# Strassen downs: where the weight sums, the g sums, two state sections and the last recombination stand in a one-core kernel

## The chip, the cores and the metric

The kernel runs on one core of a Trainium2 chip. A core has five engines that each run their own program in order: TensorE (PE, matmuls, with its weight loads shown apart as PEld), VectorE (DVE), ScalarE (ACT), GpSimd (POOL) and SyncE (SP), which here issues all loads, transposes and stores as DMAs. Engines wait for one another by semaphores only. SBUF is the on-chip memory that all engines read, PSUM the small accumulator memory of eight banks (128 x 512 float32 each) that PE writes.

The metric is the device time of one execution in microseconds (us), the median over the runs of a kernel. Profiled executions carry a span, from the first to the last recorded instruction or transfer, and all times "at 91.77" are measured from the span's start.

## The reference

Linear attention with decay over 4 batches, 8 heads, 768 positions and 64 dimensions, in blocks of 64, and then a feed-forward layer over the 3072 tokens:

```
for b in range(nb):                                   # per head, blocks of 64
    intra = ((qb @ kb.T) * Dmask) @ vb                # Dmask: lam**(i-j) below the diagonal
    inter = (qb * lam_pow) @ kv_state
    out[block b] = intra + inter
    kv_state = lam_block * kv_state + (kb * rev_pow).T @ vb
x = out as 3072 x 512
h = x @ w_in                                          # 512 x 2048
g = h * (1 / (1 + exp(-h)))                           # SiLU
return g @ w_out                                      # 2048 x 512
```

Inputs and output are float32.

## The kernel before

The tokens are cut into 24 chunks of 128 (two blocks of 64 for all eight heads; the chunks of one batch follow each other, six to a batch) and into 12 groups of 256 tokens, so group g holds chunks 2g and 2g+1. All matmul operands are cast to bf16. The order of all instructions is written by hand: the program order of the code is the order in which each engine runs its own part.

**Attention.** Chunks 0 to 3 run in an opening written out as a table of words; the later ones run in `section()` (L438 to L574). For a chunk, POOL multiplies q and k by their decays (`qb`, L364, `kb`, L365; together a "prep"), SP issues DMA transposes of them into `qt` (L390) and `kn` (L391), and PE makes scores `sp`, states `kv_ps` and outputs `op`, all in 64 x 64 matmuls recorded on L540. DVE masks the scores (`ss`, L560) and adds the states up (`total`, L570 and L572); the running state is cast to bf16 (`kvs`, by `move`: ACT L178, POOL L180 or DVE L182). Values are cast by `vcast` (`vb`, ACT). The output of a chunk is cast into `xt`. For two chunks the transposes are made on PE instead (`pe_tk`, matmuls L413, copied to `kn` by DVE). `first_state()` (L579 to L589) prepares the state for the first chunk after the opening on DVE.

**Feed-forward, up.** For each group, `ups(g, i)` for i from 0 to 7 runs eight matmuls of 128 x 256 (L604) into a PSUM bank, which gives two slices of 128 of the 2048 hidden columns for the 256 tokens of the group, and ACT applies SiLU (L609, 0.60 us each) into a tile `g`.

**Feed-forward, down.** Groups 0 and 1 use plain products (`down0`, `ffn2`, matmuls L643). Groups 2 to 11 use Strassen's scheme on halves of the tokens and of the hidden and output columns: seven products of eight matmuls each (128 x 256, L711) in place of eight. This needs sums of w_out (`weight_sum`, L669 to L677: five sums, each in two halves of 128 x 1024, on DVE, L674) and sums of g (`g_sums`, L680 to L700, after each unit, on DVE): `gd` (L693) for products 6 and 7, `gc` (L689) for product 1, `gb` (L691) for products 5 and 2. For i below 4 only `gd` is made; for i from 4 to 7 `gc`, `gb` and `gd`.

`seven(g)` (L713 to L767) runs the products in the order 3, 4, 1, 6, 5, 2, 7. Two PSUM banks hold them, `o[0]` and `o[1]`, in halves of 256 columns. After product 4, ACT copies the first half of `o[0]` to `m` (msum, L733) and DVE adds the second (L734); after 6, DVE adds product 1 (L737); products 5 and 2 are then accumulated on top of 3 and 4 in `o[0]`, so product 5 waits until msum is read out. After 2, ACT copies `o[0]` (L740) and DVE subtracts it from `m` for two quarters of the output (L741); after 7, DVE adds `o[1]` (L753). For the last group, product 7 has a tile of its own, `o_tail` (L750); four stores, one for each quarter, are issued by SP in `put` (L726).

**The order around it.** The loop over g from 2 to 10 (L907 to L939) runs eight units of `ups` and then the seven products; before the product at place 2 the loop issues preps, transposes and loads for chunks ahead, and for groups 2 and 3 a section with the scores and states of chunks 2g+2 and 2g+3; before the one at place 5 a section with the outputs of chunks 2g+2 and 2g+3 and (from group 3 on) the scores and states of the next two. Group 11 comes last with nothing behind it. Ahead of the loop, w_out arrives in six loads of 512 KB in the order 0 to 5 (two of its eight pairs of slices come later); each is cast by `cast_w` (L856 to L857, on DVE). Then come loads and preps of chunks 4 to 7, `first_state()` and the first half of the five weight sums (L865 to L866); their other half stands at L896 to L897.

`gpool` (26 buffers) holds all g tiles and g sums, each of 512 bf16 values per partition.

Of the kernel before, what the change touches and what calls it, by code (L numbers as in the profile page):

```python
# [7 lines left out]
F32 = mybir.dt.float32  # L8
# [28 lines left out]
def kernel(  # L37
# [29 lines left out]
    gpool = ctx.enter_context(tc.tile_pool(name="gpool", bufs=26))  # L67
# [370 lines left out]
    def section(outs=(), scores=(), states=(), e="AA", tags=(("att", 3),) * 2, spare=None, cast="D"):  # L438
# [126 lines left out]
        for c, h in states:  # L565
            b = c // NB
            kvs = nat.tile([128, NP, D], BF16, name="kvs", tag="kvs", bufs=8)
            old, total[b] = total.get(b), nat.tile([128, NP, D], F32, name="total", tag="total", bufs=4)
            if old is None:
                nc.vector.tensor_copy(total[b], place(c, h))  # L570
            else:
                nc.vector.tensor_tensor(total[b], old, place(c, h), op=AL.add)  # L572
            move(cast, kvs, total[b])
            kvh[(c, 1) if h == 0 else (c + 1, 0)] = kvs  # L574
# [31 lines left out]

    def ffn1_close(g, i):
        gg = gpool.tile([128, 2, 256], BF16, name="g", tag="g")
# [3 lines left out]
        gt[g, 2 * i, "pair"] = gg  # L612
# [65 lines left out]
    gs = {}  # L678

    def g_sums(g, i):  # L680

        lo, hi = slice(0, 128), slice(128, 256)
        one = gt[g, 2 * i, "pair"]
        first = i < K2 // 2
        d = gpool.tile([128, 2, 128], BF16, name="gd", tag="g", padded_shape=[128, 2, 256])
        if not first:
            low = gt[g, 2 * i - K2, "pair"]
            cross = gpool.tile([128, 2, 128], BF16, name="gc", tag="g", padded_shape=[128, 2, 256])
            nc.vector.tensor_tensor(cross, low[:, :, lo], one[:, :, hi], op=AL.add)  # L689
            both = gpool.tile([128, 2, 256], BF16, name="gb", tag="g")  # L690
            nc.vector.tensor_tensor(both, low, one, op=AL.add)  # L691
        a, b = (hi, lo) if first else (lo, hi)
        nc.vector.tensor_tensor(d, one[:, :, a], one[:, :, b], op=AL.subtract)  # L693
        for u in range(2):
            k = 2 * i + u - (0 if first else K2)
            gs[g, 6 if first else 7, k] = d[:, u, :]
            if not first:
                gs[g, 1, k] = cross[:, u, :]
                gs[g, 5, k] = both[:, u, lo]
                gs[g, 2, k] = both[:, u, hi]  # L700
# [12 lines left out]
    def seven(g):  # L713

        o = [psum.tile([128, 2, HALF], F32, name="o_ps", **bank("o")) for _ in range(2)]
        last = g == len(GROUPS) - 1
        tail = psum.tile([128, HALF], F32, name="o_tail", tag="h", bufs=2, padded_shape=[128, 512]) if last else None
        ob = pairs[g] if g < 6 else opool.tile([128, 4 * HALF], F32, name="ob", tag="ob")
        quarters = ob.rearrange("p (a n) -> p a n", a=4)
        m = work.tile([128, HALF], F32, name="msum", tag="msum", bufs=2)  # L720
        r0 = gstart[g]

        def put(rows, cols, src):
            dst = out[r0 + BLK * rows:r0 + BLK * rows + BLK, cols[0]:cols[1]]
            if last:
                nc.sync.dma_start(out=dst, in_=src)  # L726
            elif g < 6:
                held.append((dst, src))
            else:
                stores.append([0, dst, src])  # L730

        def after_4():
            nc.scalar.activation(m, o[0][:, 0, :], AF.Copy)  # L733
            nc.vector.tensor_tensor(m, m, o[0][:, 1, :], op=AL.add)  # L734

        def after_6():
            nc.vector.tensor_tensor(m, m, o[1][:, 0, :], op=AL.add)  # L737

        def after_2():
            nc.scalar.activation(quarters[:, 1:3, :], o[0], AF.Copy)  # L740
            nc.vector.tensor_tensor(quarters[:, 0::3, :], m[:, None, :].to_broadcast([128, 2, HALF]), o[0], op=AL.subtract)  # L741
            if last:
                put(0, (HALF, DM), quarters[:, 1, :])
                put(1, (0, HALF), quarters[:, 2, :])
                nc.vector.tensor_tensor(quarters[:, 3, :], quarters[:, 3, :], o[1][:, 1, :], op=AL.add)
                put(1, (HALF, DM), quarters[:, 3, :])

        def after_7():
            if last:
                nc.vector.tensor_tensor(quarters[:, 0, :], quarters[:, 0, :], tail, op=AL.add)  # L750
                put(0, (0, HALF), quarters[:, 0, :])
                return
# [4 lines left out]
        order = [(3, 0, 0, True, None), (4, 0, 1, False, after_4), (1, 1, 0, True, None), (6, 1, 1, False, after_6),  # L757
                 (5, 0, 0, False, None), (2, 0, 1, False, after_2), (7, 1, 0, True, after_7)]

        def step(n, b, x, start, after):  # L760
            def run():
                product(g, n, tail if n == 7 and last else o[b][:, x, :], start)
# [16 lines left out]
    later += [("in", 6, set()), ("in", 7, set())] + [("out", i, {f"w:{i},{a}" for a in range(2)}) for i in range(6)]  # L779
# [20 lines left out]
    def op_g(g, b, i):  # L800
        if b == 0:
            ffn1_close(g, i)
            return
        m = 4 * b + 2 * g + i
        gg = gpool.tile([128, 512], BF16, name="g", tag="g")
        nc.scalar.activation(gg, hps["m", m], AF.Silu)
        for x in range(2):
            gt[x, m] = gg[:, 256 * x:256 * x + 256]
# [47 lines left out]
    for i in range(6):  # L856
        cast_w("out", i)  # L857
    load_q(4)
# [6 lines left out]
    for i in range(len(WSUMS)):  # L865
        weight_sum(i, 0)  # L866
# [35 lines left out]
    def ups(g, i):  # L902
        ffn1_two(g, i)
        g_sums(g, i)

    many = (("h", 2),) * 2 + (("att", 3),) * 2
    for g in range(2, len(GROUPS) - 1):  # L907
        c, d, a, b = range(2 * g + 2, 2 * g + 6)
        for i in range(8):
            if g == 2 and i == 4:  # L910
                preps(8, 9)
                load_qk(10)
                transposes(8, 9)
                load_vs(8, 9)
                load_qk(11)
            if g < 4 and i in (4, 5):
                vcast(c + i % 2)
            ups(g, i)
        for i, unit in enumerate(seven(g)):
            if i == 2 and g > 2:  # L920
                vcast(a)
                if g == 3:
                    vcast(b)
            if i == 2:
# [5 lines left out]
            if i == 2 and g < 4:  # L930
# [44 lines left out]
```

## Time and profile before

| what | value |
|---|---|
| device time, median of 3 runs (lowest, highest) | 202.19 us (201.71, 202.57) |
| profiled execution: its own time | 202.42 us |
| its span | 200.6 us |
| granted TensorE clock, mean | 1.0 |
| group g=4, start of its first up to the next group's | 80.27 to 95.7 us |
| the same for g=6 and g=8 | 14.40 us each |
| six loads of w_out land at | 26.59, 27.82, 29.10, 30.45, 31.71, 32.95 us |
| last product's end, last store's landing | 196.63, 199.74 us |

Some rows of the costliest groups of instructions. A row names the line, the engine, the operation, the tiles out<-in, shapes and count, then busy us, the mean ns of one, and idle time just before them with what ended it:

```profile
L604 PE MATMUL h_ps<-xt,w_in_bf 128*128 128x256 bf16 x672 | 76.2, 272 | 0.0
L609 ACT ACTIVATE g<-h_ps 128x512 bf16<-128x512 f32 x84 | 49.9, 597 | 33.3 <-PE h_ps L604 32.1
L693 DVE TENSOR_TENSOR gd<-g 128x256 bf16<-128x256 bf16 x80 | 28.6, 376 | 5.7 <-ACT g L609 5.7
L691 DVE TENSOR_TENSOR gb<-g 128x512 bf16<-128x512 bf16 x40 | 18.5, 462 | 0.0
L689 DVE TENSOR_TENSOR gc<-g 128x256 bf16<-128x256 bf16 x40 | 13.4, 334 | 4.1 <-ACT g L609 3.5
L674 DVE TENSOR_TENSOR wsum<-w_out_bf 128x1024 bf16<-128x1024 bf16 x10 | 9.5, 1015 | 0.0
```

The mean of a duration mixes different surroundings: gd of 128 x 256 takes 0.28 us in some places and 0.70 in others. A duration includes a part that overlaps the next instruction on the same engine, so the step from one start to the next (0.20 for a gd of 0.28) is the shorter number. The chain of waits lists, for a window of time, what the last work to end was waiting on, step by step.

### The profile page before, as it was taken

How to read it: one execution, taken by the hardware profiler on the slowest of the kernel's cores; microseconds unless marked ns; L12 is line 12 of the kernel's file. 1: busy time of each engine (PE TensorE's matmuls, PEld its weight loads, DVE VectorE, ACT ScalarE, POOL GpSimd, SP SyncE). 2: the span in 40 equal slices, each digit the busy share in tenths (PEclk: the TensorE clock that was granted, in tenths of full speed). 3: DMA queues.
4: the chain of work that ended last, by engine and by line, in shares of the span. 5: the costliest groups of instructions: out<-in, count | busy, mean ns of one | idle time of the engine just before them, and what ended most of it. 6: DMA issues, size and time to landing. Idle time of an engine off the chain costs nothing.

```text
span 200.6 us, 6753 instructions
## 1 busy us (share of the span) xinstructions
PE 189.5 (94%) x2840; PEld 151.0 (75%) x2844; DVE 142.3 (71%) x333; ACT 102.5 (51%) x191; POOL 69.3 (35%) x124
## 2 busy tenths in 40 slices
PE   7789999989999998999999999999999998999992
PEld 2367544546888887887888888888888887888881
DVE  1796356999986496996995885975866857664542
ACT  3874974244825755552563563662753642634611
POOL 5240000967473141782571734705642102000000
PEclk9999999999999999999999999999999999999999
DMA  3999999999593986976887959769989991200202
GB/s 102 336 352 400 402 409 302 277 263 233 116 199 85 232 163 146 213 146 139 180 120 169 211 84 228 168 137 245 174 200 381 186 335 65 105 0 3 108 0 105
DMA packets 95582, 38.72 MB, mean 193 GB/s; under 512 B 80960, under 2 KB 88640, under 8 KB 95552
## 3 DMA queue, kind: packets, MB, share of 16 engines
q1 hardware_dynamic: 93328, 37.76, 72.9%
q10 hardware_dynamic: 2224, 0.53, 1.2%
q8 instruction: 22, 0.36, 0.7%
q14 instruction: 8, 0.07, 0.1%
HBM read 27.27 MB, written 6.29 MB: 167 GB/s over the span
## 4 chain that ended last, share of the span: by engine, by line
PE 61%; DVE 15%; DMA 13%; POOL 3%; ACT 3%; issue 2%; SPq 1%; DVEq 0%; POOLq 0%; ACTq 0%
PE h_ps L604 29%; PE o_ps L711 23%; DMA pair<-in_q_dram 6%; DMA pair<-in_moe_w_out_dram 4%; DMA pair<-in_moe_w_in_dram 4%; PE op L540 4%; DVE gd L693 3%; PE o_ps L643 3%; DVE gb L691 2%; DVE gc L689 2%; DVE total L572 2%; DVE ss L560 2%; PE sp L540 1%; ACT g L609 1%; POOL kb L365 1%
## 5 line engine op out<-in xcount | busy, mean ns | idle before, releaser
L604 PE MATMUL h_ps<-xt,w_in_bf 128*128 128x256 bf16 x672 | 76.2, 272 | 0.0
L604 PEld LDWEIGHTS <-w_in_bf 128*128 128x128 bf16 x672 | 65.4, 97 | 9.1
L609 ACT ACTIVATE g<-h_ps 128x512 bf16<-128x512 f32 x84 | 49.9, 597 | 33.3 <-PE h_ps L604 32.1
L693 DVE TENSOR_TENSOR gd<-g 128x256 bf16<-128x256 bf16 x80 | 28.6, 376 | 5.7 <-ACT g L609 5.7
L364 POOL TENSOR_TENSOR qb<-qf,lam_fwd 128x256 bf16<-128x256 f32 x18 | 12.4, 690 | 48.4 <-issue 30.3
L711 PE MATMUL o_ps<-w_out_bf,gb 128*128 128x256 bf16 x160 | 20.8, 273 | 1.4 <-issue 0.9
L711 PE MATMUL o_ps<-wsum,gd 128*128 128x256 bf16 x152 | 19.7, 273 | 0.0
L178 ACT ACTIVATE xt<-op 128x256 bf16<-128x256 f32 (+1 forms) x18 | 8.3, 486 | 21.5 <-PE op L540 21.1
L182 DVE CAST xt<-op 128x256 bf16<-128x256 f32 (+1 forms) x16 | 8.3, 542 | 15.3 <-PE op L540 13.9
L711 PE MATMUL o_ps<-wsum,g 128*128 128x256 bf16 x160 | 19.1, 273 | 0.0
L691 DVE TENSOR_TENSOR gb<-g 128x512 bf16<-128x512 bf16 x40 | 18.5, 462 | 0.0
L711 PEld LDWEIGHTS <-gb 128*128 128x128 bf16 x160 | 14.9, 98 | 3.7 <-issue 1.7
L180 POOL CAST kvs<-total 128x256 bf16<-128x256 f32 x26 | 10.5, 420 | 19.9 <-DVE total L572 16.6
L711 PEld LDWEIGHTS <-gd 128*128 128x128 bf16 x160 | 15.7, 98 | 1.8
L711 PEld LDWEIGHTS <-g 128*128 128x128 bf16 x160 | 15.7, 98 | 1.8
L689 DVE TENSOR_TENSOR gc<-g 128x256 bf16<-128x256 bf16 x40 | 13.4, 334 | 4.1 <-ACT g L609 3.5
L364 POOL TENSOR_TENSOR kb<-kf,lam_bwd 128x256 bf16<-128x256 f32 x20 | 14.2, 710 | 4.6 <-DMA kf<-in_k_dram 3.4
L572 DVE TENSOR_TENSOR total<-total,kv_ps 128x256 f32<-128x256 f32 x33 | 13.8, 418 | 2.2
L643 PE MATMUL o_ps<-w_out_bf,g 128*128 128x512 bf16 x60 | 14.1, 379 | 0.4 <-issue 0.3
L365 POOL TENSOR_TENSOR kb<-kf,lam_bwd 128x256 bf16<-128x256 f32 x20 | 14.3, 714 | 0.0
L560 DVE TENSOR_TENSOR ss<-sp,mask 128x512 bf16<-128x512 f32 x20 | 12.8, 680 | 0.0
L365 POOL TENSOR_TENSOR qb<-qf,lam_fwd 128x256 bf16<-128x256 f32 x18 | 12.1, 670 | 0.0
(95 smaller groups left out, 243.3 us busy)
## 6 DMA issues: line engine op xcount, KB each, us to landing
vf<-in_v_dram SPq DMA_DIRECT2D x20, 256.0 KB, 4.8
kf<-in_k_dram SPq DMA_DIRECT2D x19, 256.0 KB, 5.0
qf<-in_q_dram SPq DMA_DIRECT2D x17, 256.0 KB, 4.5
pair<-in_moe_w_out_dram SPq DMA_DIRECT2D x8, 512.0 KB, 7.9
pair<-in_moe_w_in_dram SPq DMA_DIRECT2D x6, 512.0 KB, 7.4
out_dram<-pair SPq DMA_DIRECT2D x12, 256.0 KB, 3.8
out_dram<-ob SPq DMA_DIRECT2D x10, 256.0 KB, 3.6
pair<-in_k_dram SPq DMA_DIRECT2D x4, 256.0 KB, 4.5
```

The source lines that it names most:

```text
L180: nc.gpsimd.tensor_copy(dst, src)
L364: eng.tensor_tensor(dst[:, 0::2], src[:, 0::2, ::-1, :], by[:, 0::2, ::-1, :], op=AL.mult)
L365: eng.tensor_tensor(dst[:, 1::2], src[:, 1::2], by[:, 1::2], op=AL.mult)
L560: nc.vector.tensor_tensor(ss, sp.rearrange("k w p q -> k (w p) q"), mask64[:, None, :].to_broadcast([128, len(scores) * NP, D]), op=AL.mult)
L572: nc.vector.tensor_tensor(total[b], old, place(c, h), op=AL.add)
L604: nc.tensor.matmul(hps[g, i][:, a:a + 256], lhsT=w_in_bf[:, ko, m * 128:(m + 1) * 128], rhs=xt[g][:, ko, :], start=(ko == 0 and u == 0), s ...
L609: nc.scalar.activation(gg.rearrange("p u n -> p (u n)"), hps[g, i], AF.Silu)
L643: nc.tensor.matmul(o, lhsT=gt[g, ko][:, mt * BLK:(mt + 1) * BLK], rhs=w_out_bf[:, ko, :], start=(ko == 0), stop=(ko == KO_OUT - 1))
L689: nc.vector.tensor_tensor(cross, low[:, :, lo], one[:, :, hi], op=AL.add)
L691: nc.vector.tensor_tensor(both, low, one, op=AL.add)
L693: nc.vector.tensor_tensor(d, one[:, :, a], one[:, :, b], op=AL.subtract)
L711: nc.tensor.matmul(dst, lhsT=lhsT, rhs=rhs, start=(start and k == 0), stop=(k == K2 - 1), skip_group_check=True)
```

## The change

Four things are changed.

1. w_out is loaded in the order 0, 1, 4, 5, 2, 3 and cast in that order, and the first half of the weight sums is made between its casts: sums 0 and 1 after cast 5, sum 2 after cast 2, sums 3 and 4 after cast 3. The loads and preps of chunks 4 to 7 and `first_state()` come behind them.
2. The SiLU outputs of two units share a tile of four slices (`quad`, 14 buffers of double size in place of 26). The g sums are made for two units at once: `g_cross` (gc of 128 x 512, gb of 128 x 1024) after units 5 and 7, `g_diff` (gd of 128 x 512) after units 1, 3 and 5; the last `g_diff` (units 6 and 7) comes after msum in `after_4`. A group has 8 such DVE instructions in place of 16.
3. For group 3, the section with the scores and states of chunks 8 and 9 that stood at place 2 issues its matmuls before unit 7; its totals and casts (`finish`) are called at place 2 of the products, after two vcasts. For group 2 the section stays.
4. In the last group the products run in the order 3, 4, 1, 6, 2, 5, 7; products 3 and 5 share a bank, 4 and 2 another, and 1, 6 and 7 have one each. The copies, subtractions, additions and stores are made quarter by quarter as their product ends.

PE keeps its 5,690 instructions and SP its 124, those in the same order; DVE's g sums fall from 160 instructions to 80.

```diff
-    gpool = ctx.enter_context(tc.tile_pool(name="gpool", bufs=26))
+    gpool = ctx.enter_context(tc.tile_pool(name="gpool", bufs=14))
...
-        for c, h in states:
...
+        def finish():
+            for c, h in states:
...
+        if defer:
+            return finish
+        finish()
...
+    def quad(*key):
+        if key not in quads:
+            quads[key] = gpool.tile([128, 4, 256], BF16, name="g", tag="g")
+        return quads[key]
...
-    def g_sums(g, i):
...
+    def g_cross(g, j):
+
+        low, one = quad(g, j - 2), quad(g, j)
+        cross = sum_tile(g, "gc", 0, 128)[:, j - 2]
+        nc.vector.tensor_tensor(cross, low[:, :, lo], one[:, :, hi], op=AL.add)
+        both = gpool.tile([128, 4, 256], BF16, name="gb", tag="g")
+        nc.vector.tensor_tensor(both, low, one, op=AL.add)
...
+    def g_diff(g, j):
+
+        one = quad(g, j)
+        d = sum_tile(g, "gd", j // 2, 128)[:, j % 2]
+        a, b = (hi, lo) if j < 2 else (lo, hi)
         nc.vector.tensor_tensor(d, one[:, :, a], one[:, :, b], op=AL.subtract)
...
+        def after_3():
+            nc.scalar.activation(m, place[3], AF.Copy)
+
         def after_4():
-            nc.scalar.activation(m, o[0][:, 0, :], AF.Copy)
-            nc.vector.tensor_tensor(m, m, o[0][:, 1, :], op=AL.add)
+            if not last:
+                after_3()
+            nc.vector.tensor_tensor(m, m, place[4], op=AL.add)
+            g_diff(g, 3)
...
+        def last_2():
+            nc.scalar.activation(quarters[:, 2, :], place[2], AF.Copy)
+            quarter(2)
+            nc.vector.tensor_tensor(quarters[:, 3, :], m, quarters[:, 2, :], op=AL.subtract)
+            nc.vector.tensor_tensor(quarters[:, 3, :], quarters[:, 3, :], place[6], op=AL.add)
+            quarter(3)
+
+        def last_5():
+            nc.scalar.activation(quarters[:, 1, :], place[5], AF.Copy)
+            quarter(1)
+            nc.vector.tensor_tensor(quarters[:, 0, :], m, quarters[:, 1, :], op=AL.subtract)
+
+        def last_7():
+            nc.vector.tensor_tensor(quarters[:, 0, :], quarters[:, 0, :], place[7], op=AL.add)
+            quarter(0)
+
+        if last:
+            order = [(3, True, after_3), (4, True, after_4), (1, True, after_1), (6, True, None),
+                     (2, False, last_2), (5, False, last_5), (7, True, last_7)]
...
-    later += [("in", 6, set()), ("in", 7, set())] + [("out", i, {f"w:{i},{a}" for a in range(2)}) for i in range(6)]
+    later += [("in", 6, set()), ("in", 7, set())] + [("out", i, {f"w:{n},{a}" for a in range(2)}) for n, i in enumerate((0, 1, 4, 5, 2, 3))]
...
-    for i in range(6):
+    for i in (0, 1, 4, 5):
         cast_w("out", i)
+    weight_sum(0, 0), weight_sum(1, 0)
+    cast_w("out", 2)
+    weight_sum(2, 0)
+    cast_w("out", 3)
+    weight_sum(3, 0), weight_sum(4, 0)
...
     first_state()
-    for i in range(len(WSUMS)):
-        weight_sum(i, 0)
...
     def ups(g, i):
         ffn1_two(g, i)
-        g_sums(g, i)
+        if i > 3 and i % 2:
+            g_cross(g, i // 2)
+        if i % 2 and i < 7:
+            g_diff(g, i // 2)
...
+            if g == 3 and i == 7:
+                late = section((), (c, d), steps(c, d), cast="A", defer=True)
             ups(g, i)
...
                 if g == 3:
                     vcast(b)
+                    late()
...
-            if i == 2 and g < 4:
+            if i == 2 and g == 2:
                 section((), (c, d), steps(c, d), cast="A")
```

More of the change, by code (lines that the diff above doesn't have):

```diff
@@ L436, with section @@
     T64 = 32
-    def section(outs=(), scores=(), states=(), e="AA", tags=(("att", 3),) * 2, spare=None, cast="D"):
+    def section(outs=(), scores=(), states=(), e="AA", tags=(("att", 3),) * 2, spare=None, cast="D", defer=False):
         jobs = {(r, x): [] for r in range(2) for x in range(2)}
@@ L678, with sum_tile @@
     gs = {}
-    def g_sums(g, i):
[L682 to L700, printed above, removed]
+    lo, hi = slice(0, 128), slice(128, 256)
+    def sum_tile(g, kind, j, width):
+        key = kind, g, j
+        if key not in quads:
+            quads[key] = gpool.tile([128, 2, 4, width], BF16, name=kind, tag="g", padded_shape=[128, 2, 4, 128])
+        return quads[key]
+    def g_cross(g, j):
[4 more added lines that the diff above has]
+        nc.vector.tensor_tensor(both, low, one, op=AL.add)
+        for u in range(4):
+            k = 4 * (j - 2) + u
+            gs[g, 1, k] = cross[:, u, :]
+            gs[g, 5, k] = both[:, u, lo]
+            gs[g, 2, k] = both[:, u, hi]
+    def g_diff(g, j):
+        one = quad(g, j)
+        d = sum_tile(g, "gd", j // 2, 128)[:, j % 2]
+        a, b = (hi, lo) if j < 2 else (lo, hi)
+        nc.vector.tensor_tensor(d, one[:, :, a], one[:, :, b], op=AL.subtract)
+        for u in range(4):
+            gs[g, 6 if j < 2 else 7, 4 * (j % 2) + u] = d[:, u, :]
     def product(g, n, dst, start):
```

64 lines of the change are left out of this document (33 added, 31 removed).

## The prediction, made before the changed kernel was run

> **What bounds the kernel now.** I read the page's first part and its chain of waits, then TensorE's (PE's) idle times one by one in the timeline, the chain around each, and SyncE's (SP's) queue.
>
> ```profile
> PE 189.5 (94%) x2840; PEld 151.0 (75%) x2844; DVE 142.3 (71%) x333; ACT 102.5 (51%) x191; POOL 69.3 (35%) x124
> PE 61%; DVE 15%; DMA 13%; POOL 3%; ACT 3%; issue 2%; SPq 1%; DVEq 0%; POOLq 0%; ACTq 0%
> ```
>
> PE is busy for 94% of a 200.6 us span at full granted clock, and both programs have the same 5,690 PE instructions. So the change can only earn PE's stalls and what follows the last matmul. After 26 us the excess gaps between PE's starts sum to 6.0 us. Those that the change can reach: 0.80 at 41.25 (transposes of L413 behind POOL's kb), 0.46 at 61.29 (states of group 2), 1.03 from 76.56 to 77.47 (states of group 3), 0.34 at 90.07 and 0.60 at 91.77 (g sums of group 4), 0.23 at 105.36 (gc of group 5). Two of 0.32 (43.30, 46.83) and one of 1.10 (167.72) follow PE's own issue; nothing here touches them.
>
> Chain of waits, 34 to 49 us and 87 to 96 us (start, us, what):
>
> ```profile
> 39.15 1.02 POOL kb L364
> 40.17 1.03 POOL kb L365
> 41.20 0.05 issue
> 41.25 0.34 PE tk L413 x3
> ...
> 90.01 0.76 DVE gb L691
> 90.77 0.62 DVE gd L693
> 91.39 0.34 DVE msum L734
> 91.73 0.04 issue
> 91.77 1.03 PE o_ps L711 x8
> ```
>
> In the first, the POOL steps are 1.02 because the weight sums run on DVE beside them (0.57 before those start). In the second, DVE works off g sums until the msum that frees a bank for PE.
>
> The end, chain of waits from 190 us and SP's queue:
>
> ```profile
> 190.51 5.25 PE o_ps L711 x48
> 195.76 0.02 issue
> 195.78 0.61 ACT ob L740
> 196.39 0.02 issue
> 196.41 0.70 DVE ob L741
> 197.11 0.02 issue
> 197.14 0.42 DVE ob L745
> 197.56 0.33 DVEq L970
> ...
> 196.41 1.98 SPq L726 DMA_DIRECT2D out_dram<-ob  x4
> ```
>
> Product 2 is done at 195.75; three instructions in a row and the last add (L750, to 197.88) follow, the last store is issued at 198.01, lands 1.73 later at 199.74, and the span ends at 200.6.
>
> **The w_out sums.** Five sums of 128x1024 leave the stretch 36.55 to 41.73. There each took a step of 1.02 beside POOL; moved between the casts, before POOL starts at 34.7, they have 0.60 each (their row's shortest step). Casts land-bound today (the six land from 26.59 to 32.95, 1.25 apart, a cast 0.69) leave 0.56 in each gap; casts 2 and 3 end at about 33.1 and 34.4, and PE wants the last at 34.98: 0.5 of cover. If sums beside POOL took 1.02 there, three would cost 1.26 and PE would wait 0.8; POOL idle until 34.7 excludes most of it. first_state (2.85) goes from 33.70 to about 36.0. kb ends near 40.0, PE's transposes follow at 40.4: −0.8 at that place. What is late next is group 2: the kvs cast behind product 4 (ACT 0.4, msum 0.41, now gd of units 6 and 7 at 0.34 to 0.75, two ss 1.28, totals 1.3, kvs 0.43) is ready at 60.95 to 61.35, against 61.24 now. So of the 0.8 only 0 to 0.3 get past group 2.
>
> **The g sums.** Per group 16 DVE instructions become 8 of twice the size. Alone gd or gc steps by 0.20, a 128x512 by 0.335 and a 128x1024 by 0.60 (the wsum row); beside POOL 0.62, 0.76, 1.02. A group alone falls from 8x0.20+4x0.20+4x0.335 = 3.74 to 6x0.335+2x0.60 = 3.21; wholly beside POOL from 10.5 to 6.6. The last gd now follows msum, so product 5's bank is free earlier. I take it that 0.34+0.60 in group 4 and 0.23 in group 5 leave PE; from group 6 to 10 there is no such stall to remove. Against that, gc of units 6 and 7 is one instruction, after the second Silu: Silu ends 0.62 after unit 7's matmuls, PE wants gc 2.06 after them, so 1.44 for 0.335 to 0.76 plus what DVE still has. Beside POOL the three sums after unit 5 take 2.54 against 1.77 until the next pair: 0.77+0.76 = 1.53, late by 0.09 in the worst case.
>
> **The section of group 3.** Its 0.67 us of score and state matmuls go ahead of unit 7, its totals and kvs casts stay behind msum, the last gd and two vcasts. The same DVE list then ends near 77.1 instead of 77.42. The rows after it need kn of chunk 11, whose transpose lands at 77.44 and is used at 77.68: 0.24 of room. Bounds for this edit: −0.3 and +0.3 (the gd and POOL); I take 0.
>
> **What the middle can keep.** SP issues loads and transposes back to back from 27 to 137 us, without a semaphore wait:
>
> ```profile
> 88.11 1.21 SPq L391 DMA_TRANSPOSE kn<-kb  x1
> 89.43 1.21 SPq L390 DMA_TRANSPOSE qt<-qb  x1
> 90.73 1.22 SPq L391 DMA_TRANSPOSE kn<-kb  x1
> 92.00 0.57 SPq L232 DMA_DIRECT2D qf<-in_q_dram  x1
> ...
> DMA to landing us min/median/max: 2.3/2.3/2.3
> ...
> 93.14 0.34 PE L540 MATMUL sp<-qt,kn 64*64 64x64 bf16 x16
> ```
>
> The kn of chunk 13 is issued at 90.73, lands at 93.04 and is first used at 93.105. A PE that comes a microsecond sooner waits there for all but 0.07. SP's rows keep their order and number (124), and are paced by themselves, so they come no sooner. For chunk 15 it is 107.40 against 107.77 (0.37), for 17 already 1.5, later over 4. So everything saved before 93 us is cut to 0.07; the gc wait of group 5 adds 0.23 and still fits in 0.37. Middle: −0.3 (0.27 to 0.37).
>
> **The tail.** The order is now 3, 4, 1, 6, 2, 5, 7, each with its bank. Product 2 ends a product (1.04) sooner; its ACT copy is 128x256 (0.385, L733's row) and its two DVE rows of 0.42 end before product 5's. After product 5 (195.59): copy to 196.0, subtraction 0.42 to 196.4. Product 7 ends 196.63, the last add (0.41) 197.07, its store goes at 197.10 instead of 198.01: −0.91. The other three stores, 0.33 to 0.43 of issue each, are out before. If the last two stores crowd SP the gain is 0.91−0.33 = 0.58; more than 0.91 isn't there, since product 7 stays last.
>
> **Sum.** −0.3 −0.9 = −1.2 on a span of 200.6 (execution 202.42, 0.23 above the runs' median of 202.19): span 199.4, median 201.0. Less than 0.5% (1.01 us) is about what a measurement of this kernel can't tell from no change.
>
> **Rivals.** (B) The transposes are no cap: a store or load that now starts elsewhere lets SP run ahead. Then group 4 gives 0.94, group 5 0.23, what is ahead of them 0.35, the tail 0.91: −2.4, 199.8. For it: the PE waits are real; against: no SP row waits for an engine.
> (C) The middle gives nothing, as the merged gc comes late where PE would have gained (0.09 a group, groups 3 to 6, against 0.3), and the tail 0.6 to 0.9: 201.3 to 201.6. For it: one sum must wait for two Silus; against: DVE has nothing else queued between units 5 and 7.
> The Trainium skill, "Perfetto Trace Analysis", section "Optimizing Scalar/DVE Operations", speaks for C: where DVE isn't saturated but causes bubbles elsewhere, it advises breaking instructions up; this change joins them. By that rule the sum would be C's, 201.3 to 201.6.
> (D) Slower: POOL loses to longer DVE rows. Place: the sixteen preps of chunks 12 to 15, each at 1.02 instead of about 0.62: 6.4 us, less POOL's idle and SP's slack there (about 1.5+0.57+0.5), puts kn of chunk 15 some 3.8 late and PE 3.4; with the tail +2.5, 204.7. It decides from 1.3 of lateness (0.24 a prep); past 0.5% from 0.30 a prep. For it: the wsum row beside kb is exactly that (1.02 each); against: DVE's two-input work beside POOL shrinks in sum, as above.
> The Trainium skill, "SBUF — State Buffer", section "Who interferes with whom", calls this an exclusive lock between a two-input DVE row and a GpSimd read; by full blocking a pair would take 0.60+0.57 = 1.17, near the 1.02 of the trace, and D's price would be 0.15 a prep higher.
>
> **Chances.** Forecast 0.50 (200.6 to 201.5), B 0.20, C 0.16, D 0.14. Faster by over 0.5% (below 201.18): most of the forecast, 0.36, and B: 0.56. Within: 0.14 of the forecast, C, 0.02 of D: 0.32. Slower: 0.12. The range 199.6 to 202.4 leaves out D, and a B that exceeds its sum.
>
> **What would show it.** PE's waits at L413 near 41 us, at msum and gc in groups 4 and 5 gone; in their place a wait of sp (L540) for kn at about 92 to 93 us with SP's times unchanged within 0.2; group 5 on 0.3 ahead. The last store issued 0.9 sooner against the end of product 7. Wrong if SP's transposes of chunks 12 to 15 shift by over 0.5, if PE waits for gc in groups 6 to 10, or if a new stall on issue appears.

## The result, and the profile after

| | before | changed |
|---|---|---|
| median of 20 runs each, us | 202.53 | 201.11 |
| lowest to highest, us | 201.65 to 205.4 | 199.86 to 203.5 |
| ratio, 95% interval | | 0.9931 [0.9911, 0.9951] |
| profiled execution, its span, us | 202.42, 200.6 | 200.34, 198.0 |

The changed kernel is 0.7% faster (1.0 to 1.8 us). Its profiled execution is 0.77 us below its own median: its run times lie in two groups, ten up to 200.84 and ten from 201.38, and the profile is of the first. So the profile's 2.6 us must not be read as the gain. Ratios here leave out executions over 1.5% above the kernel's fastest, medians take all, and the table of experiments says how many were left out.

The first and fourth part of the page after:

```profile
span 198.0 us, 6663 instructions
PE 188.5 (95%) x2844; PEld 151.1 (76%) x2844; DVE 131.2 (66%) x254; ACT 102.3 (52%) x192; POOL 71.3 (36%) x124
PE 76%; DVE 7%; DMA 5%; POOL 3%; SPq 3%; ACT 3%; issue 2%; ACTq 0%; DVEq 0%; POOLq 0%
```

DVE lost 79 instructions and 11 us; the chain's share on DVE fell from 15% to 7%. PE's waits from 26 us on (who waited for whom: us in total, times, longest), before and then after:

```profile
PE o_ps L711 <- issue: 0.9, 1, 0.9
PE tk L413 <- POOL kb L365: 0.6, 1, 0.6
PE op L540 <- ACT kvs L178: 0.6, 3, 0.2
PE o_ps L711 <- DVE msum L734: 0.4, 1, 0.4
PE o_ps L643 <- issue: 0.3, 2, 0.2
PE o_ps L711 <- DVE gc L689: 0.2, 1, 0.2
```

```profile
PE op L540 <- ACT kvs L178: 0.6, 3, 0.2
PE o_ps L729 <- issue: 0.5, 1, 0.5
PE sp L540 <- DMA kn<-kb: 0.4, 1, 0.4
```

The waits for kb, msum and gc are gone, the one for kvs is untouched, and a new one stands in their place: for the DMA transpose of kn. The two short stalls on issue at L643 are absent here too, but most of the later profiles have them, so that isn't shown to be the change's doing. SP's queue around it, and the chain of waits:

```profile
87.29 1.21 SPq L391 DMA_TRANSPOSE kn<-kb  x1
88.61 1.21 SPq L390 DMA_TRANSPOSE qt<-qb  x1
89.91 1.22 SPq L391 DMA_TRANSPOSE kn<-kb  x1
```

```profile
89.91 2.32 DMA kn<-kb
92.22 0.04 issue
92.27 0.32 PE sp L540 x16
```

Where the 2.6 us of the two profiles lie, by stretches of the span (each from the start of a group's first up to another's):

| stretch | before | changed | difference |
|---|---|---|---|
| start to group 2 | 48.34 | 47.74 | -0.60 |
| groups 2 to 4 | 47.36 | 47.04 | -0.32 |
| groups 5 to 8 | 57.99 | 57.63 | -0.36 |
| group 9 | 15.55 | 15.05 | -0.50 |
| groups 10, 11, tail | 31.36 | 30.54 | -0.82 |

Group 9 holds the stall on PE's own issue (0.94 before, 0.46 here), which the change doesn't touch. The tail, DVE and SP in the timeline:

```profile
193.47 0.43 DVE L786 TENSOR_TENSOR ob<-msum,ob 128x256 f32<-128x256 f32 x1 [1.74 <-ACT ob L784]
194.00 0.42 DVE L787 TENSOR_TENSOR ob<-ob,o_last 128x256 f32<-128x256 f32 x1
194.35 0.42 DVE L793 TENSOR_TENSOR ob<-msum,ob 128x256 f32<-128x256 f32 x1
194.88 0.42 DVE L796 TENSOR_TENSOR ob<-ob,o_last 128x256 f32<-128x256 f32 x1
```

Product 7 ends at 194.77; the last add starts 0.11 behind it, since three DVE rows run back to back from product 2 on. From the last product to the end, with the spans to two places: 196.62 to 200.59 = 3.97 before, 194.77 to 197.97 = 3.20 after: -0.77.

### The profile page after: what moved, and what is told of

Read it like the earlier page. It is cut to its first block, busy times and chain, and to the rows that moved or that the text cites. A ratio compares the mean times of both kernels' runs of the same rounds, so it can differ in the third digit from the quotient of the medians.

```text
span 198.0 us, 6663 instructions
## 1 busy us (share of the span) xinstructions
PE 188.5 (95%) x2844; PEld 151.1 (76%) x2844; DVE 131.2 (66%) x254; ACT 102.3 (52%) x192; POOL 71.3 (36%) x124
## 3 DMA queue, kind: packets, MB, share of 16 engines
q1 hardware_dynamic: 93328, 37.76, 75.8%
## 4 chain that ended last, share of the span: by engine, by line
PE 76%; DVE 7%; DMA 5%; POOL 3%; SPq 3%; ACT 3%; issue 2%; ACTq 0%; DVEq 0%; POOLq 0%
PE h_ps L609 32%; PE o_ps L729 23%; PE o_ps L654 6%; PE h_ps L843 5%; PE op L540 3%; SPq L224 2%; DMA pair<-in_q_dram 2%; PE o_last L729 2%; DVE ss L560 2%; PE sp L540 1%; DVE total L573 1%; DMA qf<-in_q_dram 1%; DMA kn<-kb 1%; ACT g L621 1%; POOL kvs L180 1%
## 5 line engine op out<-in xcount | busy, mean ns | idle before, releaser
L364 POOL TENSOR_TENSOR qb<-qf,lam_fwd 128x256 bf16<-128x256 f32 x18 | 12.0, 667 | 40.5 <-issue 25.4
L716 DVE TENSOR_TENSOR gd<-g 128x512 bf16<-128x512 bf16 x40 | 20.5, 515 | 8.2 <-ACT g L621 8.0
L180 POOL CAST kvs<-total 128x256 bf16<-128x256 f32 x26 | 11.0, 433 | 25.6 <-DVE total L573 20.0
L729 PE MATMUL o_ps<-w_out_bf,gb 128*128 128x256 bf16 x144 | 18.9, 273 | 0.5 <-issue 0.5
L729 PE MATMUL o_ps<-wsum,gd 128*128 128x256 bf16 x144 | 18.7, 273 | 0.0
L702 DVE TENSOR_TENSOR gc<-g 128x512 bf16<-128x512 bf16 x20 | 9.7, 484 | 13.2 <-ACT g L621 13.2
L729 PE MATMUL o_ps<-wsum,g 128*128 128x256 bf16 x144 | 17.2, 273 | 0.0
L364 POOL TENSOR_TENSOR kb<-kf,lam_bwd 128x256 bf16<-128x256 f32 x20 | 14.6, 731 | 3.9 <-DMA kf<-in_k_dram 2.9
L704 DVE TENSOR_TENSOR gb<-g 128x1024 bf16<-128x1024 bf16 x20 | 15.9, 798 | 0.0
L654 PE MATMUL o_ps<-w_out_bf,g 128*128 128x512 bf16 x64 | 15.0, 379 | 0.1
L365 POOL TENSOR_TENSOR kb<-kf,lam_bwd 128x256 bf16<-128x256 f32 x20 | 14.4, 718 | 0.0
L365 POOL TENSOR_TENSOR qb<-qf,lam_fwd 128x256 bf16<-128x256 f32 x18 | 13.0, 721 | 0.0
```

The lines of the kernel that those rows point to most:

```text
L180: nc.gpsimd.tensor_copy(dst, src)
L364: eng.tensor_tensor(dst[:, 0::2], src[:, 0::2, ::-1, :], by[:, 0::2, ::-1, :], op=AL.mult)
L365: eng.tensor_tensor(dst[:, 1::2], src[:, 1::2], by[:, 1::2], op=AL.mult)
L654: nc.tensor.matmul(o, lhsT=gt[g, ko][:, mt * BLK:(mt + 1) * BLK], rhs=w_out_bf[:, ko, :], start=(ko == 0), stop=(ko == KO_OUT - 1))
L729: nc.tensor.matmul(dst, lhsT=lhsT, rhs=rhs, start=(start and k == 0), stop=(k == K2 - 1), skip_group_check=True)
```

## The experiments

Times vary by 1 to 2 us between executions of one kernel, so a ratio's interval is about as wide as what is asked for, and most conclusions rest on a wait in the trace of one execution.

| kernel | runs, left out of the ratio | median us | ratio to before, interval | span of its profile |
|---|---|---|---|---|
| tail alone | 12, 0 | 201.34 | 0.9947 [0.992, 0.9973] | 199.5 |
| all but the tail | 12, 0 | 201.30 | 0.9931 [0.9896, 0.9965] | 199.0 |
| w_out sums as before | 12, 0 | 201.49 | 0.9951 [0.9919, 0.9983] | 200.3 |
| load of chunk 14 later | 12, 1 | 201.28 | 0.9932 [0.9907, 0.9958] | 199.0 |
| 60 PE instructions more at the start | 10, 3 | 201.53 | 0.9919 [0.9874, 0.9964] | 198.7 |
| g sums per unit | 6, 2 | 200.87 | 0.9888 [0.9832, 0.9944] | 197.7 |
| section of group 3 as before | 12, 0 | 201.56 | 0.9959 [0.9926, 0.9993] | 199.5 |
| three edits | 6, 3 | 202.63 | 0.9892 [0.9828, 0.9957] | 204.9 |
| changed kernel again | 12, 4 | 201.18 | 0.9902 [0.9856, 0.9947] | 198.4 |
| three edits again | 6, 3 | 201.92 | 0.9892 [0.9832, 0.9952] | 201.2 |
| four edits | 12, 7 | 203.35 | 0.9967 [0.9915, 1.002] | 200.9 |
| shift in group 8 | 12, 1 | 200.53 | 0.9906 [0.987, 0.9942] | 198.6 |

**The tail alone, and all but the tail.** The first is the kernel before with the new `seven` (without `g_diff` in `after_4`), the second the changed kernel with the old one:

```diff
-        order = [(3, 0, 0, True, None), (4, 0, 1, False, after_4), (1, 1, 0, True, None), (6, 1, 1, False, after_6),
-                 (5, 0, 0, False, None), (2, 0, 1, False, after_2), (7, 1, 0, True, after_7)]
+            order = [(3, True, after_3), (4, True, after_4), (1, True, after_1), (6, True, None),
+                     (2, False, last_2), (5, False, last_5), (7, True, last_7)]
```

> The kernel before with the last group's new order, banks and quarter copies alone; all else as before. Theory (tail and middle add up, and the last group is independent of the rest): from the end of product 7 to the end of the span 3.23 us as in the changed kernel, against 3.98 before, so 0.75 us or 0.37% faster than before (ratio 0.996). Rival 1 (the prediction's own figure): 0.91. Rival 2 (the tail only looks shorter because its stores end on a clearer queue): under 0.3 us. The waits for kb at 41, for msum and gc in groups 4 and 5 stay as before in all of them.

> The changed kernel with the last group as before (order 3, 4, 1, 6, 5, 2, 7, one copy of 128x512, one subtraction of 128x512). Theory: PE's products end within 0.3 us of the changed kernel's 194.77, and what follows the last product is 3.98 us again; 0.6 to 0.7 us faster than before, all of it from the middle. Rival (the middle gains only the 0.3 that was predicted, and the rest of the profile's difference is chance between runs): 0.3 us faster than before, not to be told from it.

From the last product to the end: 3.19 us with the new tail alone (196.30 to 199.49), 3.98 with the old tail (195.07 to 199.05). In the traces the tail is worth 0.78 in both directions, wherever the rest stands, so neither 0.91 nor under 0.3. The times are coarser: the ratio is 0.9931 with the whole change and also with all but the tail. All but the tail is 0.7 to 2.1 us faster than before, so the rival's 0.3 falls; its products end at 195.07, 0.30 behind the changed kernel's, although its stall in group 9 was longer (an excess of 1.70 over PE's usual step, against 0.62). One thing was not expected. In the first kernel the middle is that of before, yet msum and gc don't wait in group 4:

```profile
PE o_ps L711 <- issue: 1.4, 1, 1.4
PE op L540 <- ACT kvs L178: 0.6, 3, 0.2
PE sp L540 <- DMA kn<-kb: 0.5, 1, 0.5
PE tk L413 <- POOL kb L365: 0.3, 1, 0.3
PE o_ps L643 <- issue: 0.3, 2, 0.2
```

There DVE's sums of group 4 were through at 88.8, when POOL's prep of chunk 14 had just begun (88.37); in the profile before, four of them ran beside it from 88.69 on, at 0.70 to 0.83 each. So the 0.94 us that the prediction saw in group 4 belong to that execution; here PE waits for kn of chunk 13 in their place (0.68).

**w_out sums as before.**

```diff
-    for i in (0, 1, 4, 5):
+    for i in range(6):
         cast_w("out", i)
-    weight_sum(0, 0), weight_sum(1, 0)
-    cast_w("out", 2)
-    weight_sum(2, 0)
-    cast_w("out", 3)
-    weight_sum(3, 0), weight_sum(4, 0)
...
     first_state()
+    for i in range(len(WSUMS)):
+        weight_sum(i, 0)
```

> The changed kernel with the order of the w_out loads, casts and weight sums as before. Theory (group 2's states and then the transposes of chunk 13 take back what the front gains): PE waits for kb at L413 again, 0.6 to 0.8, group 2 starts about 0.6 later than in the changed kernel, but the wait for kvs in group 2 (0.65) and the one for kn at 92 (0.54) shrink, and from group 5 on the difference to the changed kernel is under 0.2 us. Rival (the front's gain is kept to the end): 0.6 us slower than the changed kernel, all groups shifted alike.

The wait for kb is back (0.57 excess), and from the first up to group 2 it takes 30.89 against 30.49. But the transposes of chunk 13 were late as well (issued at 91.56), PE waited 1.20 for kn, and group 5 began 1.66 later than in the changed kernel's profile. The wait for kvs in group 2, which the theory wanted smaller, was about 1.0 against 0.65. The theory's "under 0.2" isn't borne out by this execution; the medians differ by 0.4, within their noise. Whether the front's 0.4 are kept to the end stays open.

**The load of chunk 14 behind the transposes of 12 and 13.**

```diff
-                load_qk(*([12] if g == 2 else []), c + 7)
+                load_qk(*([12] if g == 2 else [14] if g == 3 else []), c + 7)
                 load_vs(c + 6, d + 6)
-                load_qk(d + 7)
+                if g > 2:
+                    load_qk(d + 7)
```

> The changed kernel with one load pair (q and k of chunk 14) issued by SP behind the transposes of chunks 12 and 13 in place of ahead of them. Theory (the wait for kn at 92.27, 0.54 excess, is the cap on the middle): kn of chunk 13 lands 1.5 to 2 us sooner, the wait is gone, group 5 starts 0.3 to 0.55 us sooner against the changed kernel, and so does the end unless kn of chunk 15 takes it back. Rival (kn is late for POOL's or DVE's sake and not for SP's queue): kn lands where it did and nothing changes. Second rival: chunk 14's preps come late and kn of chunk 15 costs as much as was won.

kn of chunk 13 was issued at 88.38 and landed at 90.75, 2.4 us ahead of its first use at 93.14, and no row of the waits names kn:

```profile
PE op L540 <- ACT kvs L178: 0.8, 4, 0.2
PE o_ps L729 <- issue: 0.5, 1, 0.5
PE o_ps L654 <- issue: 0.3, 2, 0.2
```

Groups 2 to 4 took 46.57 against 47.04, about the wait of 0.54. Counted from the start of group 4, kn of chunk 13 is issued after 7.0 us here (after 4.0 to 7.8 in the four later profiles with this edit) and after 8.4 to 10.7 in the nine profiles with the old order. That fits the theory that the order in SP's queue sets it. That the edit removed the wait is not shown: PE came late itself in this execution (group 4 began at 81.41 against 79.87), and six of the nine profiles with the old order have no wait for this kn either. The opening was 1.5 us longer here than in the changed kernel's profile; the granted clock reads 0.50 from 16.8 to 20.2 us. The median shows no gain.

**60 PE instructions more at the start.**

```diff
-            fill(wt, n)
+            wt = wt.rearrange("p a b -> p (a b)")
+            for x in range(2 * n if n > 4 else n // 2):
+                w = 128 if n > 4 else 512
+                nc.tensor.matmul(wt[:, 0:w], lhsT=zero[:, :BLK], rhs=zero[:, 0:w], start=True, stop=True, skip_group_check=True)
```

> The changed kernel with the ten warm-up matmuls of 128x512 on zeros at the start written as forty of 128x128: 60 PE instructions more, the same zero columns, ahead of any data. Theory (the PE stalls on issue at 15.6 and 165.2 are fetches of PE's program: a 16 KB packet of the instruction queue starts 2.4 to 2.6 us before PE goes on in each of six profiles, and in group 9 exactly where a section of 256 short instructions begins, so that it is used up in 1.2 us): shifting the program by 60 instructions puts the boundary into the middle of that section and the stall of 0.62 to 1.70 is gone; the one at 15.6 (0.9) gets smaller or stays; 0.6 to 1.9 us faster than the changed kernel, and the two clusters of its run times (about 200.4 and 201.6) become one. Rival (the stall belongs to the stores that SP issues from 157 to 161 and not to the place of the boundary): the stall stays at 165 to 168 or moves by less than 1 us.

The chain of waits in group 9, before, and after, each with the stall on issue:

```profile
166.45 0.33 PE o_ps L711 x2
166.78 0.94 issue
167.72 1.69 PE o_ps L711 x14
```

```profile
165.15 0.32 PE o_ps L729 x2
165.47 0.46 issue
165.93 1.69 PE o_ps L729 x14
```

With the shift neither this nor the stall of 0.85 at 16.5 is there; PE's waits of that kernel from 26 us on:

```profile
PE op L540 <- ACT kvs L178: 0.8, 4, 0.2
PE o_ps L654 <- issue: 0.3, 2, 0.2
PE o_ps L729 <- DVE gc L702: 0.3, 1, 0.3
```

Group 9 takes 14.43 instead of 15.05. Over all fourteen profiles the stall (excess of PE's start gap) is 0.58 to 1.70 in all nine profiles with the old program position and absent in all five with a shifted one. Its size goes with the stores: where SP issues the last of the burst ahead of it 8.1 to 8.7 us after group 9's start, it is 0.58 to 0.67 (four profiles); at 9.4 to 11.9, 1.05 to 1.70 (five). The difference is about the gap between the two groups of run times, but that the upper group is this was not shown. So whether there is a stall depends on the place of the boundary, and not on the stores as the rival has it; its size seems to depend on them. The time didn't follow (0.9919 against 0.9931), and the two groups of times did not become one: seven runs lie from 199.5 to 201.88, three from 203.36 to 207.6. In the profile the stall's gain is given back early: group 2 starts at 48.61 against 47.74 (the granted clock reads 0.50 from 10.9 to 17.7 us), and gc costs 0.45 in group 3. What made the three long runs is not known, as none of them was profiled.

**g sums per unit.** `g_cross` and `g_diff` are replaced by sums after each unit on the same tiles, with gd of units 6 and 7 ahead of msum:

```diff
-        if i > 3 and i % 2:
-            g_cross(g, i // 2)
-        if i % 2 and i < 7:
-            g_diff(g, i // 2)
+        g_sums(g, i)
...
-            g_diff(g, 3)
```

> The changed kernel with the g sums per unit again (16 DVE instructions a group, gd of units 6 and 7 ahead of msum). Theory (what larger sums win is given back at the wait for kn in group 4): a wait for gc or msum in group 4 may come back, up to 0.94, if POOL's prep of chunk 14 meets the sums, and then the kn wait of group 5 shrinks by as much; group 5 starts within 0.3 of the changed kernel's, groups 6 to 10 run as long (14.4 each), the time is within 0.3 us. Rival (merging is worth its own stalls): group 5 starts 0.9 later and the time is 0.9 to 1.2 us longer.

The ratio is 0.9888 [0.9832, 0.9944]: not slower than the changed kernel. Its waits show gc once in group 3 (0.77 excess), then 0.17 to 0.19 for msum in groups 4 and 7 and for gc in group 8, and no 0.94. Group 5 begins at 94.28 against 94.78, which is more than the theory's 0.3, and groups 7 and 8 take 0.2 to 0.3 longer each, which it didn't foresee. The rival (0.9 to 1.2 longer) falls: merging the sums, the largest edit of the change, has no gain that these runs can show. Two of its six runs took 203.62 and 203.76 us, so long runs come with the old program position as well.

**The section of group 3 as before.** `late` is removed and the condition at place 2 is `g < 4` again.

> The changed kernel with the state section of group 3 issued whole at place 2 of the products again. Theory (the deferral earns little: kvs comes at 76.9 against 77.4 and kn of chunk 11 lands at 77.27 anyway): waits for kvs in group 3 of 0.8 to 1.1 in place of 0.75, group 4 starts 0 to 0.3 later, the end within 0.2 us of the changed kernel's. Rival: the deferral is what keeps group 3's DVE list in time; without it group 3 loses over 0.6 us, and group 5 over 0.5.

The kvs waits of group 3 are 0.42, 0.33 and 0.42 in place of 0.33 and 0.42, so the deferral saves some 0.4 of waiting in this pair of profiles (1.17 in sum against 0.75; 0.8 to 1.1 was expected). Group 3 took 17.71 against 16.54, but 0.97 of that is PE waiting for a SiLU that ACT held behind a vcast whose load landed late. The ratio (0.9959) is higher than the changed kernel's by less than the intervals; theory and rival are not told apart.

**Three edits, twice, and four.** The 60 instructions, the later load, and, for groups 2 and 3, the last gd at place 3 of the products, behind the state sums. The fourth is the vcasts of group 3 at units 5 and 6 instead of 4 and 5.

```diff
+            if i == 3 and g < 4:
+                g_diff(g, 3)
...
-            if g < 4 and i in (4, 5):
-                vcast(c + i % 2)
+            if g < 4 and i in (g + 2, g + 3):
+                vcast(c + i - g - 2)
```

> The changed kernel with three edits: the 60 PE instructions of the first run of this series, the load of chunk 14 behind the transposes of chunks 12 and 13, and in groups 2 and 3 the last gd behind the state sums (product 7 wants it last). Theory (caps taken in order: fetch, kn, kvs): the fetch stall is gone (0.6 to 1.7), kn no longer waits in group 4, kvs comes 0.33 sooner in groups 2 and 3, of which 0.1 to 0.2 stay in group 3 before kn of chunk 11: 1.0 to 2.4 us faster than the changed kernel. Rival (each cap hides another): only the fetch stall's share shows.

> The changed kernel once more, unaltered, beside the next two on the same chip. Theory (what differs between its executions is the moment at which DMAs land, and with it two waits: the fetch of PE's program in group 9, 0.6 to 1.7, and kn of chunk 13 in group 4, 0 to 1.2): kn of chunk 13 is issued somewhere from 88.8 to 91.6, and the sum of the two waits explains where this execution's span lies between 198 and 199.6; ratio to before 0.991 to 0.995 again. Rival: another place varies, and the span moves without these two.

> The kernel with the three edits once more (60 PE instructions more in the warm-up, chunk 14's load behind the transposes of 12 and 13, the last gd behind the state sums in groups 2 and 3). Theory: no stall on issue at 165 to 168, no wait for kn in group 4, products end 0.6 to 2.0 us sooner than in the unaltered changed kernel beside it, median 0.5 to 1.5 us lower. Rival (each cap hides another): the same median within 0.3 us.

> The three edits and, in group 3, the two vcasts of chunks 8 and 9 one unit later in ACT's queue (at units 5 and 6): they wait for loads that land from 67.5 to 69.2 and hold the SiLU of the next units behind them, which cost PE 0.16, 0.30, 0.97 and 1.52 in four of the profiles. Theory: no wait of ups for a SiLU in group 3, 0 to 0.5 us better on the median than the three edits, and fewer long runs. Rival: the state section of group 3, which needs both, then waits for vb, and it is as long or longer.

The changed kernel again gave the ratio 0.9902, a fetch stall of 1.05 (0.62 in the first profile), and kn of chunk 13 issued at 88.88 with no wait for it (0.54). The two sums, 1.05 and 1.16, don't order the spans, 198.4 and 198.0, as the theory wanted: gc cost 0.33 and 0.35 in groups 3 and 4 here, so a third place varies. The three edits ran at 199.50, 199.72 and 201.76 us, and at 203.49, 203.55 and 207.34; the second time at 199.86, 200.19 and 200.50, and at 203.33, 203.65 and 206.06. The four edits ran from 199.89 to 204.88, seven of twelve above 203. So the medians lie 0.7 to 2.2 us above the changed kernel's, where 0.5 to 2.4 less was forecast for the three edits. The fourth edit brought no fewer long runs, though its profile has no wait for a SiLU in group 3, as forecast.

The stall in group 9 is gone in all three profiles. But in all three PE waits some 3 us in group 3 for kn of chunk 11. The chain of waits of the repeat:

```profile
74.98 0.03 issue
75.01 4.12 DMA kn<-kb
79.13 0.04 issue
79.18 0.26 PE sp L540 x2
```

DMA traffic from 75 to 77.3 us, its queues and its issues (count, us to landing):

```profile
q8 instruction: 1, 0.02, 4.7%
...
kn<-kb SPq DMA_TRANSPOSE x1, 4.1
```

A fetch of PE's program (q8) starts at 76.01 here, inside the transpose; in the changed kernel at 78.96, behind it. So a fetch met the transpose that group 3 waits for. The 60 instructions alone don't do that: the profile with only them has the fetch at 79.53, its kn landed 2.3 us after its issue, and PE didn't wait for it. Counted from the start of group 3, the fetch starts 13.5 us in here against 15.0 there, and kn is issued at 12.5 against 10.4: PE is earlier, as the later gd is meant to have it, and SP's queue later.

Nor is the fetch all of the wait: without it, at 2.3 us to landing in place of 4.12, kn would have landed at 77.3, and PE was ready at 76.15; so some 1.8 of the 3.0 us go with the fetch (an estimate from these rows). Group 3 loses more than the wait, too: the granted clock reads 0.50 from 77.7 to 84.5 us, the 16 matmuls of products behind the section take 3.53 us against 1.85 in the changed kernel, and group 3 takes 21.31 against 16.54. The other two profiles show such a stretch as well (80.4 to 83.8 and 81.0 to 87.8). Both theories missed this, and the fourth edit is buried under it. The three profiles are of executions of 207.34, 203.65 and 203.27 us; none near 200 us was taken, so whether those lack the wait isn't shown.

**The shift in group 8.** Load and gd as above, the warm-up as in the changed kernel, and in product 7 of group 8:

```diff
+            if g == 8 and n == 7 and k == K2 - 1:
+                for _ in range(18):
+                    nc.tensor.matmul(dst[0:64, 0:64], lhsT=zero[0:64, 0:64], rhs=zero[0:64, 0:64], start=False, stop=False, skip_group_check=True)
```

> The changed kernel with chunk 14's load behind the transposes of 12 and 13, the last gd behind the state sums in groups 2 and 3, and the program shifted late: 18 pairs of 64x64 matmuls on zeros (36 PE instructions) in product 7 of group 8 in place of the 60 in the warm-up. Theory (a fetch of PE's program that falls between issue and landing of a transpose delays it: 4.1 us against 2.3 in the twelve profiles so far, 59 and 228 transposes; the 60 instructions in the warm-up moved the fetch of group 3 from 79 to 76, onto kn of chunk 11, and cost 3.0 there): fetches up to group 8 stand as in the changed kernel, kn of chunk 11 lands 2.3 after its issue, no wait of 3 us in group 3; the boundary in group 9 falls inside the section and the stall at 165 to 168 is gone; the 36 instructions cost 0.3. Median 0.5 to 1.5 us under the changed kernel's 201.1, ratio to before 0.986 to 0.991, and no cluster at 203. Rival (the 3 us in group 3 come from the later gd or the moved load): kn of chunk 11 is late again, a cluster at 203 stays.

The count in that expectation comes from thirteen profiles, not twelve. DMA traffic of this kernel from 75.8 to 78.1 us, where its kn of chunk 11 is issued, has no q8 row, and

```profile
kn<-kb SPq DMA_TRANSPOSE x1, 2.3
```

The wait of 3 us is gone, kn costs 0.35 and 0.33 in groups 2 and 3, the granted clock is not halved in the middle, the stall in group 9 is gone (group 9 takes 14.43), and eleven of twelve runs lie from 199.14 to 201.54, one at 202.72. The trace is not a clean test of the 3 us, though: in group 3 PE waits 1.4 us for a SiLU that ACT held behind a vcast, which stands ahead of kn's use, so PE came to kn later. The 18 pairs took 0.68, not 0.3, and group 8 with them 15.30 against 14.35. With the median at 200.53 and ratio 0.9906 [0.987, 0.9942] it is faster than before; that it beats the changed kernel's 0.9931 is not shown.

## Why the prediction was right, and where not

The forecast was 201.0 and -1.2 us; 201.11 and -0.7% (1.0 to 1.8 us) came out. Direction and size hold, the split doesn't quite. That the median was met to 0.1 us is partly luck: the forecast started from 202.19, the median of three runs, where twenty gave 202.53, and it expected 1.2 of gain where 1.4 came; the two misses offset each other.

**Tail, -0.91.** Right in mechanism, 0.14 too much. The sum let the last add follow product 7 at once; DVE's three rows before it run back to back, so it starts 0.11 later than product 7's end instead of 0.03, and the store leaves 0.58 after that end, not 0.47. Issue to landing and landing to end stayed within 0.05 of before.

**The wait that takes the place.** Right: PE arrives sooner in group 4 and waits for kn of chunk 13 (0.54), in the unchanged middle of the first experiment too (0.68); with one load moved from ahead of it kn came sooner, counted from group 4, and PE didn't wait, though that execution doesn't prove it was the move.

**The cap of 0.07.** This is the step that failed: "SP's rows keep their order and number (124), and are paced by themselves, so they come no sooner." One execution's landing was taken for a constant. The sign that the prediction gave for being wrong here, a shift of SP's transposes of chunks 12 to 15 by over 0.5, is there: kn of these four was issued 0.8 to 2.6 us sooner in the profile after. kn of chunk 13 landed 0.82 sooner, and over nine profiles with the same order of loads and transposes it is issued between 88.83 and 91.56, a spread of 2.7 us. So the shift lies within what executions differ by, and it isn't shown that the change made it. Whether PE is early or late doesn't explain it: the earliest two have group 4 beginning at 79.58 and 79.64, but 89.72 goes with 81.29 and 89.91 with 79.87. So the middle's gain isn't cut to 0.3 always, it is cut by what the transposes of that execution allow: 0.92 by group 5 in the profile after. The medians leave about 0.65 for it (1.42 less the tail's 0.77), and all but the tail was 0.7 to 2.1 us faster than before. Which of the edits in the middle earns this stays open: w_out sums, g sums and section of group 3 were each undone alone, and no ratio tells the result from the changed kernel's.

**Group 4's 0.94 and group 5's 0.23** were priced from one profile. The first experiment, with those sums unchanged, had neither, and the kernel with sums per unit only 0.18 in their place; the price of such a stall depends on whether POOL's prep meets DVE's sums, which differed between these executions.

**The front, -0.8 with 0 to 0.3 past group 2.** Right: group 2 starts 0.60 sooner, group 3 only 0.27, and the kvs wait of group 2 grew from 0.32 to 0.65.

**The section of group 3 at nothing:** its kvs waits went from 1.03 to 0.75 in the profile after, within the bounds of 0.3 either way.

**"Nothing here touches" the stall of 1.10 at 167.72.** True of the code. But it is the part that differs most between executions (0.58 to 1.70), and 0.48 of the profiles' difference is its chance.

Of the rivals, B (transposes that come sooner) has its sign in the profiled execution, and its 199.8 is near that one, not near the median; PE still waited for kn. C's lateness of gc did occur (0.33 to 0.45 in group 3 in three profiles), yet with the sums per unit gc was late by 0.77 there, so the merge isn't shown as its cause, and undoing the merge isn't faster or slower by what can be measured. By the Trainium skill, "Perfetto Trace Analysis", section "Optimizing Scalar/DVE Operations", breaking up may let work complete sooner; the runs neither confirm nor refuse it (0.9888 [0.9832, 0.9944] against 0.9931 [0.9911, 0.9951]). D didn't happen: kn of chunk 15 was issued at 102.65, 2.4 sooner than before, and POOL's prep rows of chunks 12 to 15 take 0.62 to 1.06, most of them 0.62.

## What to carry to other kernels

A wait in one profile is a sample: before it is priced, see what releases it and how much that moves between executions; here a transpose's issue moved by 2.7 us, and PE's wait for it was anything from 0 to 1.2 us. What follows the last matmul was the safest gain: its 0.78 came out in the trace of either kernel it was put on. When a stall reads "issue" at the entrance or inside a run of very short matmuls, look for a 16 KB packet of the instruction queue just ahead of it, and count instructions before moving anything.

## What the runs showed of the hardware

**PE's program is fetched in 16 KB packets, and a dense section can outrun it.** In the nine profiles with the stall in group 9, PE goes on 2.2 to 2.8 us after such a packet starts. In group 9 of the changed kernel the fetch starts at 163.39, with PE at its 4,791st instruction; a section of 64x64 matmuls begins there, its 256 instructions are used up in 1.2 us, and PE stops at the 5,056th, 1.9 us after the start of the fetch. Sixty instructions ahead of it, or 36, end the stall. The Trainium skill, "Runtime: NRT & Kernel Launch", section "Instruction fetch mechanics", says that blocks of 16 KiB (256 instructions) are fetched one ahead and that the crossing is mostly hidden; the sizes agree, and in group 9 it is not hidden, since those 1.9 us are less than the 2.5 that the fetch takes there.

**A DMA transpose that meets such a fetch lands later.** Over all fourteen profiles, of the transposes whose issue took no longer than 1.3 us, the 248 without the start of a fetch in the 2.3 us behind their issue take a median of 2.34 us to land, the 64 with one 4.11. For kn of chunk 11 the landing was 4.12 and 3.80 us behind its issue in the two profiles of the three edits, with a fetch, and 2.31 with the shift in group 8, without one. What in the DMA makes it so the traces don't show.

**A long wait of PE came with a halved clock.** In the three profiles in which PE waited some 3 us for kn, and in no other, the granted clock falls to 0.50 in the middle of the run, for 3.4 to 6.8 us during or behind that wait.
